# All value gathers as indirect transfers of GpSimd, registers read in one block, scratch in halves and block-diagonal V in place: block-sparse attention and a gated MLP

## The chip, the cores and the metric

The kernel runs on one core of one Trainium2 chip. The metric is device microseconds (us) of a run; most runs of one kernel on one chip lie within 1.5% of each other. A run is flagged slow when it is over 1.5% above the fastest of its kernel. The medians below are of all runs; the ratios leave out what was flagged slow within their rounds. The engines are called by the names of the profile: PE is TensorE, DVE is VectorE, ACT is ScalarE, POOL is GpSimd, SP is SyncE; "SPq" is the queue from which SyncE starts DMA transfers. The experiments ran on several chips, numbered here as the runs list them. Times are compared only with runs of the same kernels on the same chip, unless the text says that two chips are set side by side.

## The reference, cut to what matters

```python
# q, k, v: (4 batches, 8 heads, 768, 64) float32; blocks of 32 tokens; 24 blocks
mask = np.abs(blk_i - blk_j) <= 1                     # the window
mask |= first or last block, as query or as key       # the global blocks
for qb in range(24):
    for kb in sampled_blocks[qb]:                     # 3 random blocks each, known only at run time
        mask[qb*32:(qb+1)*32, kb*32:(kb+1)*32] = True
attn_out = softmax(where(mask, q @ k.T / 8, -1e9)) @ v
x = attn_out as (4, 768, 512)
u, v2 = split(gelu(x @ w_in)); v2 = layernorm(v2) * g_ln
out = x + (u * (w_sg @ v2 + b_sg)) @ w_out
```

What matters here is the random blocks. For each of 22 query blocks of each batch, 3 blocks of keys and 3 of values must be fetched by numbers that are in memory only.

## The kernel before

Each batch has 22 "value gathers", 88 in all: 96 rows of V for one query block, from a copy of V in DRAM (`scr`) to one of the slots of the tile `VR`. Two thirds of them are indirect transfers that GpSimd makes from row numbers in the tile `IDX`. Each third one is made of three ordinary transfers of SyncE, whose addresses come from registers.

```python
spset = list(range(2, 23, 3))          # the query blocks whose values SyncE gathers
...
if i in spset:
    def ga(e, i=i, rg=rg):
        if b == 0:
            load_regs(e, (0, 1, 2), "JSP", i)        # registers read just before use
            vals["SP", i] = vals["JSP"]
        return [e.dma_start(VR[32*j:32*j+32, rg, ...], src[bass.ds(vals["SP", i][j][0], 32), :]) for j in range(3)]
else:
    def ga(g, i=i, rg=rg):
        return g.indirect_dma_start(out=VR[0:96, rg, ...], in_=src[:, :],
                                    in_offset=bass.IndirectOffsetOnAxis(ap=IDX[0:96, i:i + 1], axis=0))
def kc(x, i=i, rg=rg):                               # the keys of the same blocks, copied on chip by VectorE
    if b == 0:
        load_regs(x, (0, 1), "JIT", i)               # just before use
        vals["DVE", i] = vals["JIT"]
    ...
```

The two global value blocks lie in `VG`, in each batch loaded whole by two transfers and then made block-diagonal by four fills of VectorE:

```python
for m in range(2):
    op("SP", f"vg{b}.{m}{hh}", ... ap(VG[bp], 64*m, 64, vo, [[1, w]]) <- whole rows ...)
def vones(x):
    x.memset(VG[bp][0:64, :, 64:65], 1.0)
    x.memset(VG[bp][64:128, :, 129:130], 1.0)
    x.memset(VG[bp][0:64, :, 65:130], 0.0)
    return x.memset(VG[bp][64:128, :, 0:65], 0.0)
```

An automatic list scheduler orders the operations of each engine by estimated times and priorities.

The softmax here doesn't subtract the row's maximum and nothing guards it: scores larger than these inputs give would overflow.

## Time and profile before

| | before |
|---|---|
| time, median of 3 runs | 299.96 us (298.42 to 302.66) |
| span of the profiled run, mean granted clock of PE | 294.7 us, 0.959 |
| PE busy, POOL busy | 223.0 us, 127.8 us |
| first attention matmul starts | 28.59 us |
| gathers of GpSimd, of SyncE | 60, 28 |

The first lines are of the page: busy time, share of the span, count of instructions.

```profile
PE 223.0 (76%) x3525; PEld 160.2 (54%) x3525; DVE 166.1 (56%) x480; ACT 149.4 (51%) x222; POOL 127.8 (43%) x224
...
PE 41%; DMA 15%; DVE 13%; POOL 10%; issue 8%; ACT 7%; SPq 3%; another core or an unknown queue 2%; DVEq 0%; ACTq 0%
```

No engine is full; the second line, the chain of waits by engine, passes through nearly all. The next lines are of the list of PE's waits (the longest, 8.8 us at the start, is among those left out): what PE was to run, what released it, us in total, times, the longest.

```profile
PE Ops L352 <- DVE VG L577: 5.3, 2, 4.4
...
PE Ops L352 <- issue: 4.5, 8, 1.2
PE Mps L352 <- DVE vh L874: 4.4, 2, 3.6
PE Mps L352 <- DVE VG L577: 4.1, 1, 4.1
...
PE Sps L352 <- issue: 2.8, 5, 1.1
```

The waits for `VG` and `vh` are what the change is after.

These two are of the groups of instructions (count, busy us and mean ns of one, then idle time before them) and of the waits of SyncE's queue.

```profile
L616 POOL DMA_INDIRECT VR<-scr,IDX x60 | 57.6, 960 | 35.1 <-PE Ops L352 13.6 <-issue 13.0 <-DMA scr<-VA 4.6
```

```profile
SPq L611 <- PE Ops L352: 32.9, 6, 14.5
```

A gather takes GpSimd about 0.92 us when it follows another, and 0.30 us pass between two. SyncE stands 33 us before its gathers until slots of `VR` are free. Last, VectorE's timeline at the start (start, duration, what, and the idle time before it):

```profile
9.09 0.18 DVE L423 CAST IDX<-Mps 96x24 int32<-96x24 f32 x1 [0.36 <-PE Mps L421]
19.61 0.49 DVE L584 MEMSET VA<- 32x520 bf16 x1 [10.35 <-DMA scr<-VA]
20.78 0.56 DVE L496 CAST qn<-x_tok 128x768 bf16<-128x768 f32 x1
```

VectorE idles 10.35 us there. This is the gap into which the change puts the reading of the registers.

### The profile page before, as it was taken

What the parts mean: (1) busy time and instruction counts of PE and PEld (TensorE: products, weight loads), DVE (VectorE), ACT (ScalarE), POOL (GpSimd) and SP (SyncE); (2) the same over time, 40 slices, a digit from 0 to 9 for tenths busy, and PEclk for the clock granted to TensorE, in tenths of its full rate; (3) what the DMA queues carried; (4) which work ended last, traced back from release to release, by engine and by line L of the source; (5) the groups of instructions that cost most, each with busy time, mean ns of one, the idle gap of its engine ahead of it and who ended that gap; (6) DMA issues with size and microseconds to landing.
All of it is one profiled execution on the core that took longest, in us unless ns stands there. A gap on an engine that the chain in (4) does not pass through costs nothing.

```text
span 294.7 us, 8583 instructions
## 1 busy us (share of the span) xinstructions
PE 223.0 (76%) x3525; PEld 160.2 (54%) x3525; DVE 166.1 (56%) x480; ACT 149.4 (51%) x222; POOL 127.8 (43%) x224
## 2 busy tenths in 40 slices
PE   0234569798899649597884897888868978999984
PEld 0123347576576327475662575666554766767542
DVE  7129432466746734335772875448646665556783
ACT  2760656783568103478554365684371755846100
POOL 1028455632643756632787547335880253003000
PEclk9999999869999989799999799999995999999999
DMA  8999686898768965596797177874830134030023
GB/s 155 266 277 245 166 260 155 185 219 212 167 135 190 265 178 140 144 259 151 168 252 172 42 144 185 173 183 148 270 110 1 29 91 127 6 110 0 0 108 108
DMA packets 87883, 45.66 MB, mean 155 GB/s; under 512 B 65924, under 2 KB 81700, under 8 KB 87844
## 3 DMA queue, kind: packets, MB, share of 16 engines
q1 hardware_dynamic: 83092, 34.79, 50.1%
q0 software_dynamic: 4752, 10.32, 13.5%
q8 instruction: 28, 0.46, 0.7%
q14 instruction: 11, 0.09, 0.1%
HBM read 36.76 MB, written 9.52 MB: 157 GB/s over the span
## 4 chain that ended last, share of the span: by engine, by line
PE 41%; DMA 15%; DVE 13%; POOL 10%; issue 8%; ACT 7%; SPq 3%; another core or an unknown queue 2%; DVEq 0%; ACTq 0%
PE Mps L352 21%; PE Ops L352 10%; PE Sps L352 7%; DMA ST<-in_v_dram 6%; POOL VR L616 5%; DMA ST<-in_q_dram 4%; PE Mps L842 3%; DVE gt L903 3%; DVE xg L906 2%; SPq L485 2%; DMA x_tok<-in_q_dram 2%; ACT PW L702 2%; ACT PR L701 2%; DMA uT<-in_k_dram 2%
## 5 line engine op out<-in xcount | busy, mean ns | idle before, releaser
L616 POOL DMA_INDIRECT VR<-scr,IDX x60 | 57.6, 960 | 35.1 <-PE Ops L352 13.6
L352 PE MATMUL Mps<-w_sgT,vh 128*128 128x384 bf16 x192 | 39.0, 351 | 11.7 <-DVE vh L874 4.4
L630 DVE COPY KR<-KT 128x128 bf16 x176 | 30.4, 232 | 19.3 <-issue 10.3
L701 ACT ACTIVATE PR<-Sps 96x1024 bf16<-96x1024 f32 (+1 forms) x24 | 22.8, 948 | 32.3 <-PE Sps L352 17.9
L634 POOL COPY KR<-KT 128x128 bf16 x88 | 24.1, 311 | 34.7 <-PE Sps L352 24.3
L702 ACT ACTIVATE PW<-Sps,b_odd 128x512 bf16<-128x512 f32 (+1 forms) x24 | 15.6, 649 | 33.6 <-PE Sps L352 21.1
L352 PEld LDWEIGHTS Mps<-w_sgT,vh 128*128 128x128 bf16 x192 | 17.9, 103 | 26.4 <-DVE VG L577 4.5
L903 DVE SCALAR_TENSOR_TENSOR gt<-Mps,gcol,bsg 128x384 f32<-128x384 f32 x32 | 19.7, 617 | 19.7 <-PE Mps L352 17.3
L352 PE MATMUL Mps<-w_out,xg 128*128 128x512 f32 x96 | 28.4, 426 | 2.4 <-DVE xg L906 1.6
L352 PE MATMUL Mps<-w_in,xg 128*128 128x512 f32 x96 | 26.7, 424 | 1.7 <-ACT QT L539 0.9
L352 PE MATMUL Mps<-xg,w_in 128*128 128x384 f32 x128 | 25.6, 352 | 3.0 <-ACT vg L861 1.8
L352 PEld LDWEIGHTS Mps<-xg,w_in 128*128 128x128 f32 x128 | 21.0, 188 | 7.6 <-ACT vg L861 2.9
L921 DVE TENSOR_TENSOR x_tok<-Mps,x_tok 128x512 f32<-128x512 f32 x24 | 16.5, 687 | 12.3 <-PE Mps L352 9.0
L352 PEld LDWEIGHTS Mps<-w_out,xg 128*128 128x128 f32 x96 | 16.9, 194 | 8.9 <-DVE xg L906 2.2
L845 ACT ACTIVATE xg<-Mps 128x512 fp32r<-128x512 f32 x24 | 14.3, 596 | 14.7 <-PE Mps L842 13.3
L352 PEld LDWEIGHTS Mps<-w_in,xg 128*128 128x128 f32 x96 | 17.4, 197 | 7.9 <-ACT vg L861 2.4
L352 PE MATMUL Ops<-VA,PW 128*64 128x65 bf16 x384 | 20.6, 206 | 1.5 <-issue 1.4
L861 ACT ACTIVATE vg<-Mps 128x512 f32<-128x512 f32 x24 | 13.9, 597 | 14.7 <-PE Mps L352 10.1
L888 ACT ACTIVATE uT<-Mps 128x384 f32<-128x384 f32 x32 | 15.7, 491 | 10.1 <-PE Mps L352 8.1
L352 PE MATMUL Ops<-VG,PG 128*128 128x130 bf16 x96 | 10.9, 238 | 12.6 <-DVE VG L577 5.3
L352 PEld LDWEIGHTS Ops<-VA,PW 128*64 128x64 bf16 x384 | 16.5, 119 | 6.2 <-issue 3.2
L863 DVE BATCH_NORM_STATS2 lnst<-vg 128x6 f32<-128x512 f32 x24 | 16.2, 677 | 6.0 <-ACT vg L861 5.9
(95 smaller groups left out, 392.5 us busy)
## 6 DMA issues: line engine op xcount, KB each, us to landing
out_dram<-x_tok SPq DMA_DIRECT2D x20, 256.0 KB, 3.5
ST<-in_k_dram SPq DMA_DIRECT2D x12, 384.0 KB
ST<-in_q_dram SPq DMA_DIRECT2D x12, 384.0 KB
ST<-in_v_dram SPq DMA_DIRECT2D x12, 384.0 KB
scr<-VA SPq DMA_DIRECT2D x4, 780.0 KB, 4.8
VR<-scr SPq DMA_DIRECT2D x84, 32.5 KB
VS<-scr SPq DMA_DIRECT2D x4, 650.0 KB
w_in<-in_moe_w_in_dram POOLq DMA_DIRECT2D x1, 2048.0 KB
```

Source lines behind the costliest of these rows:

```text
L352: return pe.matmul(o, l, r, start=start, stop=True, skip_group_check=True)
L616: return g.indirect_dma_start(out=VR[0:96, rg, v0:v1, :].rearrange("p h e -> p (h e)"), out_offset=None, in_=src[:, :], in_offset=bass.Ind ...
L630: ins = x.tensor_copy(KR[:, c0:c0 + n, rg, 32 * j:32 * j + 32], KT[:, c0:c0 + n, bass.ds(vals["DVE", i][j][0], 32)])
L634: op("POOL", f"kp{b}.{i}{hh}", lambda x, i=i, rg=rg: x.tensor_copy(KR[:, c0:c0 + n, rg, 64:96], KT[:, c0:c0 + n, bass.ds(vals["POOL"][0][i ...
L701: return lambda a: a.activation(o, i_, ACT.Exp, scale=SCALE)
L702: return lambda a: a.activation(o, i_, ACT.Exp, bias=bias[0:p1, 0:1], scale=SCALE)
L845: op("ACT", f"xE{b}.{tau}", lambda a: a.activation(xg[c][:, :, tc * P:tc * P + P], Mps[:, u.slot * 512:u.slot * 512 + 512].rearrange("p (a ...
L861: op("ACT", f"gV{b}.{tau}", lambda a: a.activation(vg[vr][:, :], Mps[:, u.slot * 512:u.slot * 512 + 512], ACT.Gelu_apprx_tanh), r=[("vp", ...
L863: op("DVE", f"bs{b}.{tau}", lambda x: x.bn_stats(lnst[:, vr, :], vg[vr][:, :]), r=[("vg", vr)], w=[("lnst", vr)], dur=0.73, prio=pr - 300)
L888: o = op("ACT", f"gU{b}.{c}{dt}", lambda a: a.activation(uT[c][:, dt, :], Mps[:, u.slot * 512:u.slot * 512 + 384], ACT.Gelu_apprx_tanh), r ...
L903: op("DVE", f"g1{b}.{c}{dt}", lambda x: x.scalar_tensor_tensor(gt[gr][:, :], Mps[:, u.slot * 512:u.slot * 512 + 384], gcol[:, dt:dt + 1], ...
L921: op("DVE", f"res{b}.{tau}", lambda x: x.tensor_tensor(x_tok[bp][:, tau, :], Mps[:, u.slot * 512:u.slot * 512 + 512], x_tok[bp][:, tau, :] ...
```

## The change

Its intent: take work off SyncE's queue and off VectorE's busy stretches. All 88 value gathers go to GpSimd. VectorE reads its 44 registers in one block in its idle time at the start. The copy of V to scratch goes in two halves, in batch 0 on ScalarE's queue. The zeros and ones of `VG` are set once for all, and transfers write only its diagonal. Some fills, evictions and orders of batch 0 move too. The diff, cut to its core:

```diff
-    spset = list(range(2, 23, 3))
+    spset = []
...
+    def regs_dve(x):
+        for i in range(1, 23):
+            load_regs(x, (0, 1), ("DVE", i), i)
+        return x.memset(lnt[0][:, :], 0.0)
+    op("DVE", "regsD", regs_dve, r=["IDX"], w=["regD", "lnt0"], dur=10.0, prio=-160)
...
             def kc(x, i=i, rg=rg):
-                if hh == 1 or b == 0:
-                    load_regs(x, (0, 1), "JIT", i)
-                if hh == 0 and b == 0:
-                    vals["DVE", i] = vals["JIT"]
...
-            hold["sc"] = op("SP", f"sc{b}.{hh}", ... dstr[0:768, :] <- VA ...)
+            for z in range(2):
+                o = op("ACT" if b == 0 else "SP", f"sc{b}.{z}", ... scr[0:768, 260 * z:260 * z + 260] <- VA[...4 * z:4 * z + 4...])
             for m in range(2):
-                op("SP", f"vg{b}.{m}{hh}", ... ap(VG[bp], 64 * m, 64, vo, [[1, w]]) ...)
-            def vones(x):                       # four fills of VG in each batch
+                op("SP", f"vg{b}.{m}", ... ap(VG[bp], 64 * m, 64, 65 * m, [[130, 4], [1, 64]]) ...)
...                                              # cut: fills of VG, VA at the start, table warm-up, batch 0's evictions
```

More of the change, by code (lines that the diff above doesn't have):

```diff
@@ L22 @@
 G2 = "DVE"
+EQA = 2
+XE0 = "DVE"
 ORD0 = "vkq"
@@ L357, in c_ident @@
     def c_ident(g):
+        g.memset(lnt[2][:, :], 0.0)
         g.memset(ident[:, :], 0.0)
         return g.memset(ident_f[:, :], 0.0)
-    op("POOL", "ident0", c_ident, w=["id0"], dur=0.4, prio=-200)
+    op("POOL", "ident0", c_ident, w=["id0", "lnt2"], dur=0.4, prio=-200)
     def c_ident1(g):
@@ L372, in bass_bigbird_attn__then__gmlp_full_block_kernel, with c_preV, c_preV1 @@
     op("POOL", "iota", c_iota, w=["iota"], dur=0.4, prio=-180)
+    def c_preV(vx):
+        ins = None
+        for i in range(2):
+            ins = vx.memset(VA[i][:, :, :, 64:65], 1.0)
+        return ins
+    op("DVE", "preV", c_preV, w=["preV"], dur=0.25, prio=-210)
+    def c_preV1(vx):
+        ins = None
+        for i in range(2):
+            vx.memset(VA[i][0:32, 0, :, 64:65], 0.0)
+            ins = vx.memset(VA[i][96:128, 5, :, 64:65], 0.0)
+        return ins
+    op("DVE", "preV1", c_preV1, r=["preV"], w=[("VA", i, h) for i in range(2) for h in range(4)], dur=0.3, prio=-205)
     def c_pre(vx):
@@ L377, in c_pre @@
         for i in range(2):
-            vx.memset(VA[i][:, :, :, 64:65], 1.0)
             vx.memset(KG[i][:, :, :], 0.0)
+            vx.memset(VG[i][:, :, :], 0.0)
         return vx.memset(KT[:, :, 768:800], 0.0)
-    op("DVE", "pre0", c_pre, w=["pre0"], dur=0.8, prio=-200)
+    op("DVE", "pre0", c_pre, w=["pre0"], dur=1.4, prio=-200)
     def c_pre1(vx):
@@ L386, in c_pre1 @@
         for i in range(2):
-            vx.memset(VA[i][0:32, 0, :, :], 0.0)
-            vx.memset(VA[i][96:128, 5, :, :], 0.0)
+            vx.memset(VG[i][0:64, :, 64:65], 1.0)
+            vx.memset(VG[i][64:128, :, 129:130], 1.0)
         vx.memset(PW[3][0:32, 0:520], 0.0)
@@ L391, in c_pre1, with dv @@
         return vx.memset(KR[:, :, :, 96:128], 0.0)
-    op("DVE", "pre1", c_pre1, r=["pre0"], w=["bias", "KTz"] + [("KG", i, c) for i in range(2) for c in range(4)] + [("VA", i, h) for i in range(2) for h in range(4)]
-       + [("KR", i, j, h) for i in range(NRING) for j in range(3) for h in range(2)] + ["PW3", "lnt3"], dur=1.2, prio=-190)
+    op("DVE", "pre1", c_pre1, r=["pre0"], w=["bias", "KTz"] + [("KG", i, c) for i in range(2) for c in range(4)]
+       + [("VG", i, m, c) for i in range(2) for m in range(2) for c in range(4)]
+       + [("KR", i, j, h) for i in range(NRING) for j in range(3) for h in range(2)] + ["PW3", "lnt3"], dur=1.6, prio=-190)
+    op("ACT", "warm", lambda a: a.activation(lnt[2][:, :], lnt[2][:, :], ACT.Exp), r=["lnt2"], w=["lnt2"], dur=1.6, prio=-200, mode="exp")
     op("SP", "sbi", lambda e: e.dma_start(sbi[:, :], sampled_blocks.bitcast(I32)), w=["sbi"], dur=0.6, prio=-300,
        dsem="c0", nbytes=600)
-    def dv(name, fn, r=(), w=(), dur=0.08, prio=-170):
+    def dv(name, fn, r=(), w=(), dur=0.17, prio=-170):
         op("DVE", name, fn, r=r, w=w, dur=dur, prio=prio)
@@ L418, in ixr @@
         return ins
-    dv("ix10", ixr, ["q3", "iota"], ["effr"], dur=0.25)
+    dv("ix10", ixr, ["q3", "iota"], ["effr"], dur=0.55)
     u_ix = Unit("M")
@@ L450, in d_scz @@
         return z
-    op("SP", "scz", d_scz, r=["PW3", ("PW", 3, 0), ("PW", 3, 1)], w=["scz"], dur=0.5, prio=-60, dsem="z0", nbytes=33000, nd=3 if SPLIT else 1)
+    op("ACT", "scz", d_scz, r=["PW3", ("PW", 3, 0), ("PW", 3, 1)], w=["scz"], dur=0.5, prio=-110, dsem="z0", nbytes=33000, nd=3 if SPLIT else 1)
     WP = -45
     def d_g(e):
+        for i in spset:
+            load_regs(e, (0, 1, 2), ("SP", i), i)
         with nc.allow_non_contiguous_dma(reason="tiny gain layout"):
@@ L458, in bass_bigbird_attn__then__gmlp_full_block_kernel @@
     hold = {"small": []}
-    op("SP", "gcol", d_g, w=["gcol"], dur=0.6, prio=WP, dsem="c1", nbytes=2e4)
+    hold["gcol"] = op("SP", "gcol", d_g, r=["IDX"], w=["gcol"], dur=5.3, prio=-92.5, dsem="c1", nbytes=2e4)
     hold["small"] += [op("SP", "bsg0", lambda e: e.dma_start(bsg[:, 0:736], moe_b_sg[32:768].partition_broadcast(P)), w=["bsg0"], dur=0.6, prio=WP, dsem="c2", nbytes=4e5)]
@@ L505, in loads @@
         for n_, (nm, c) in enumerate(od):
-            aft = [hold["sc"]] if hh else []
+            aft = []
             if b == 1:
@@ L511, in loads @@
             if b == 0 and nm == "q":
-                hold.setdefault("ldq", []).append(o)
+                o.seq.append(hold["gcol"])
+            if b == 0 and nm == "k":
+                hold["gcol"].seq.append(o)
     def transposes(b, hh):
@@ L529, in transposes @@
                 op("PE", f"TR{nm}{b}.{c}", tr, r=[(nm + "n", c), "ident"], w=[("trp", nm, b, c)], dur=0.42, prio=pr + c, mode="128", alloc=u, pre=tk)
-                ee = "ACT" if (nm == "q") == (b > 0) else "DVE"
+                ee = "ACT" if (nm == "q") == (b > 0) or (b == 0 and c >= EQA) else "DVE"
                 def ev(x, nm=nm, u=u, TT=TT, c=c, ee=ee):
@@ L558, in vprep @@
             vk = [("VA", bp, c) for c in hs]
-            dstr = scr if n == 4 else scrh[hh]
-            sk = "scr" if n == 4 else ("scrh", hh)
-            hold["sc"] = op("SP", f"sc{b}.{hh}", lambda e, dstr=dstr, c0=c0, n=n: e.dma_start(
-                dstr[0:768, :].rearrange("(t p) c -> p t c", p=P), VA[bp][:, :, 2 * c0:2 * c0 + 2 * n, :].rearrange("p t h e -> p t (h e)")),
-               r=vk, w=[sk], dur=0.5, prio=pr, dsem=f"sc{hh}", nbytes=199680 * n)
-            if b == 0 and hh == 0:
-                for o in hold["ldq"]:
-                    o.seq.append(hold["sc"])
@@ L567, in vprep @@
-            w = 130 * n
-            vo = 2 * c0 * 65
-            for m in range(2):
-                op("SP", f"vg{b}.{m}{hh}", lambda e, m=m, dstr=dstr, vo=vo, w=w: e.dma_start(
-                    ap(VG[bp], 64 * m, 64, vo, [[1, w]]), bass.AP(dstr.tensor, 0, [[736 * w, 2], [w, 32], [1, w]])),
-                   r=[sk], w=[("VG", bp, m, c) for c in hs], dur=0.5, prio=pr + 2, dsem=f"vg{m}{hh}", nbytes=66560)
-            def vones(x):
-                x.memset(VG[bp][0:64, :, 64:65], 1.0)
-                x.memset(VG[bp][64:128, :, 129:130], 1.0)
-                x.memset(VG[bp][0:64, :, 65:130], 0.0)
-                return x.memset(VG[bp][64:128, :, 0:65], 0.0)
@@ L578, in vprep @@
-            op("DVE", f"vo{b}.{hh}", vones, w=[("VG", bp, m, c) for m in range(2) for c in hs], dur=0.5, prio=pr + 2)
-            op("SP", f"vs{b}.{hh}", lambda e, dstr=dstr, vo=vo, w=w: e.dma_start(
-                ap(VS, 0, P, vo, [[520, 5], [1, w]]), bass.AP(dstr.tensor, 64 * w, [[w, P], [P * w, 5], [1, w]])),
-               r=[sk], w=[("VS", c) for c in hs], dur=0.5, prio=pr + 1, dsem=f"vs{hh}", nbytes=166400 * n)
-            def vz(x, c0=c0, n=n):
-                x.memset(VA[bp][0:32, 0, 2 * c0:2 * c0 + 2 * n, :], 0.0)
-                return x.memset(VA[bp][96:128, 5, 2 * c0:2 * c0 + 2 * n, :], 0.0)
@@ L586, in vprep @@
-            op("DVE", f"vz{b}.{hh}", vz, w=vk, dur=1.0, prio=pr + 2)
+            sk = [("scr", z) for z in range(2)]
+            for z in range(2):
+                o = op("ACT" if b == 0 else "SP", f"sc{b}.{z}", lambda e, z=z: e.dma_start(
+                    scr[0:768, 260 * z:260 * z + 260].rearrange("(t p) c -> p t c", p=P),
+                    VA[bp][:, :, 4 * z:4 * z + 4, :].rearrange("p t h e -> p t (h e)")),
+                    r=[("VA", bp, 2 * z), ("VA", bp, 2 * z + 1)], w=[("scr", z)], dur=0.65, prio=pr - 40, dsem=f"sc{z}{'a' if b == 0 else ''}", nbytes=399360)
@@ new lines, in vprep @@
+            for m in range(2):
+                op("SP", f"vg{b}.{m}", lambda e, m=m: e.dma_start(
+                    ap(VG[bp], 64 * m, 64, 65 * m, [[130, 4], [1, 64]]), bass.AP(scr.tensor, 65 * m, [[736 * 520, 2], [520, 32], [130, 4], [1, 64]])),
+                    r=sk, w=[("VG", bp, m, c) for c in hs], dur=0.7, prio=pr + 1, dsem=f"vg{m}", nbytes=131000)
+            op("SP", f"vs{b}", lambda e: e.dma_start(
+                ap(VS, 0, P, 0, [[520, 5], [1, 520]]), bass.AP(scr.tensor, 64 * 520, [[520, P], [P * 520, 5], [1, 520]])),
+               r=sk, w=[("VS", c) for c in hs], dur=0.6, prio=pr + 2, dsem="vs", nbytes=665600)
@@ L588, in bass_bigbird_attn__then__gmlp_full_block_kernel, with vz @@
+            def vz(x):
+                x.memset(ap(VA[bp], 0, 32, 0, [[1, 520]]), 0.0)
+                return x.memset(ap(VA[bp], 96, 32, 2600, [[1, 520]]), 0.0)
+            op("DVE", f"vz{b}.{hh}", vz, w=vk, dur=0.6, prio=pr + 2)
     rgof = {}
@@ L596, in gather @@
             pr = -20 + tau + 6 * hh
-        src = scr if n == 4 else scrh[hh]
-        sk = "scr" if n == 4 else ("scrh", hh)
+        src = scr
+        sk = [("scr", z) for z in range(2)]
         v0, v1 = 2 * c0, 2 * c0 + 2 * n
@@ L607, in ga @@
                 def ga(e, i=i, rg=rg):
-                    if b == 0:
-                        load_regs(e, (0, 1, 2), "JSP", i)
-                        vals["SP", i] = vals["JSP"]
                     return [e.dma_start(VR[32 * j:32 * j + 32, rg, v0:v1, :].rearrange("p h e -> p (h e)"),
                                         src[bass.ds(vals["SP", i][j][0], 32), :]) for j in range(3)]
-                ng_.append(op("SP", f"ga{b}.{i}{hh}", ga, r=[sk, "scz", "IDX"], w=vk, dur=2.8 if b == 0 else 1.9, prio=pr, dsem=f"vs{rg}h", nbytes=24960 * n, nd=3))
+                ng_.append(op("SP", f"ga{b}.{i}{hh}", ga, r=sk + ["scz", "IDX"], w=vk, dur=1.9, prio=pr, dsem=f"vs{rg}h", nbytes=24960 * n, nd=3))
             else:
@@ L617, in ga @@
                                                 in_offset=bass.IndirectOffsetOnAxis(ap=IDX[0:96, i:i + 1], axis=0))
-                ng_.append(op("POOL", f"ga{b}.{i}{hh}", ga, r=[sk, "scz", "IDX"], w=vk, dur=1.12, prio=pr, dsem=f"vs{rg}s", nbytes=24960 * n))
+                ng_.append(op("POOL", f"ga{b}.{i}{hh}", ga, r=sk + ["scz", "IDX"], w=vk, dur=1.12, prio=pr, dsem=f"vs{rg}s", nbytes=24960 * n))
             def kc(x, i=i, rg=rg):
                 ins = None
-                if hh == 1 or b == 0:
-                    load_regs(x, (0, 1), "JIT", i)
-                if hh == 0 and b == 0:
-                    vals["DVE", i] = vals["JIT"]
                 for j in range(2):
-                    if hh == 1:
-                        ins = x.tensor_copy(KR[:, c0:c0 + n, rg, 32 * j:32 * j + 32], KT[:, c0:c0 + n, bass.ds(vals["JIT"][j][0], 32)])
-                        continue
                     ins = x.tensor_copy(KR[:, c0:c0 + n, rg, 32 * j:32 * j + 32], KT[:, c0:c0 + n, bass.ds(vals["DVE", i][j][0], 32)])
@@ L632, in gather @@
             kk = [("KT", c) for c in hs] + ["KTz"]
-            op("DVE", f"kr{b}.{i}{hh}", kc, r=kk + ["IDX"], w=[("KR", rg, j, h) for j in range(2) for h in hk], dur=1.05 if b == 0 else 0.55, prio=pr)
+            op("DVE", f"kr{b}.{i}{hh}", kc, r=kk + ["regD"], w=[("KR", rg, j, h) for j in range(2) for h in hk], dur=0.55, prio=pr)
             op("POOL", f"kp{b}.{i}{hh}", lambda x, i=i, rg=rg: x.tensor_copy(
@@ L844, in mlp_x, with xev @@
         op("PE", f"xT{b}.{tau}", tr, r=[("x", bp, tau, 0), ("x", bp, tau, 1), "ident"], w=[("xp", b, tau)], dur=0.62, prio=pr, mode="128", alloc=u)
-        op("ACT", f"xE{b}.{tau}", lambda a: a.activation(
-            xg[c][:, :, tc * P:tc * P + P], Mps[:, u.slot * 512:u.slot * 512 + 512].rearrange("p (a c) -> p a c", c=P), ACT.Copy),
+        xe = XE0 if b == 0 else "ACT"
+        def xev(x):
+            o_, i_ = xg[c][:, :, tc * P:tc * P + P], Mps[:, u.slot * 512:u.slot * 512 + 512].rearrange("p (a c) -> p a c", c=P)
+            return x.tensor_copy(o_, i_) if xe == "DVE" else x.activation(o_, i_, ACT.Copy)
+        op(xe, f"xE{b}.{tau}", xev,
            r=[("xp", b, tau)], w=[("xg", c, tc)], dur=0.6, prio=pr, use=u)
```

## The prediction

> **What bounds it now.** The page shows TensorE busy for 223 of 294.7 us; no engine is near 100%. The windows of 10 us put TensorE's idle 72 us at about 24 before the first attention matmul (28.6 us), 8 in 30-60, and stalls at the heads of later batches. In the chain of waits and the timelines the change touches three:
> - batch 1, 103.7-108.1: 4.4 us on the memsets of VG, which wait behind two VG copies issued at 96.96 that seem to land near 107;
> - batch 2, 158.8-162.9: 4.1 us, same cause;
> - batch 3, 218.4-222.1: 3.6 us for vh, whose GpSimd part (lny) stands behind value gathers.
>
> The chain also runs through loads of q and v into ST (9%): the SyncE queue stands 33 us waiting for gather slots (waits of the DMA queue), with next-batch loads behind.
>
> **What changes.**
> 1. VG: the memsets (0.06+0.06+0.28+0.28 us, four times) go; the transfer writes only the diagonal. Matmuls wait for it alone; it is issued before VS, with no gathers behind it. It has 512 rows of 128 bytes instead of 128 of 1040. The Trainium skill ("DMA: Bandwidth & Descriptors", Specifications) puts line rate at 512 bytes or more; no run here shows what narrow rows cost. I expect it to land earlier anyway: TensorE gets back about 8.5 us.
> 2. All 28 SyncE gathers (84 DMAs) become GpSimd ones: 0.92 us busy + 0.30 us issue each, +34 us in all; busy 127.8 -> about 155 us. GpSimd has the room, but a refill of four slots takes 4.9 us in series instead of about 3: I charge 3.5 us of new waits. SyncE is free for loads, so q and v of batches 1-3 come several us earlier.
> 3. By the instruction order, lny of batches 1-3 now stands before the gathers: 3.6 us come back in batch 3.
> 4. Registers: 44 loads in one block on VectorE. Before, two loads cost the 0.60 us gap before each pair of KR copies (22 times, 13 us); in the block I expect 0.30 each, 13 us, from about 8.5 to 21.5 us, where VectorE idled 10.35 us. But q's casts stand behind it, so the first attention matmul comes at 27-30 us, hardly before today's 28.6.
> 5. Scratch in halves on ScalarE's queue: first gather about 2 us earlier (19.7 -> 17.5).
> 6. Batch 0: x evictions move to VectorE (+3.6 us); ScalarE has one pair of table loads less (2 x 1.28 us). w_in is issued after 16 gathers instead of 8 (32.6 -> about 40 us) and may hold the first w_in matmuls up to 3 us.
>
> **Sum.** Gains 8.5 (VG) + 3.6 (vh) + 2 (batch 0) + 2 (loads); costs 3.5 (serial gathers) + 1.5 (w_in). Net -11 us: **289 us**, 8 in 10 within **281 to 297**. Faster by over 2%: 0.76; within 2%: 0.20; slower: 0.04.
>
> **Signs.** No memset of VG after the start; no TensorE wait for it over 1 us; GpSimd about 155 us busy with 88 gathers; no SyncE wait for gather slots; first attention matmul at 27-30 us; register block about 13 us; TensorE busy near 223 us.
>
> **What would make it wrong.** Serial gathers holding the value matmuls (releaser shown as unknown queue) or the casts behind them; the narrow VG transfer landing as late as before; the register block lasting well over 13 us and delaying q. Or the reverse: early loads closing more of the 20-odd us of load waits on the chain, giving 280 or less.

## More of the kernel before

The attention itself is many short matmuls (`Sps<-QT,KR`, 32 columns; `Sps<-QT,KT`, 64; `Ops<-VA,PW` and `Ops<-VR,PR`, 65), each with a weight load of its own.

The lines with "issue" are idle time in which PE waited for nothing that the profile shows. All such lines of this kernel together come to 9.1 us.

## The result, and the profile after

The changed kernel took **345.79 us** (median of 4 runs, 343.2 to 347.03), beside 299.28 us for the kernel before (4 runs). The ratio of the fast runs is 1.152, with a 95% interval of 1.141 to 1.163. Such a ratio, here and below, is the mean time of one kernel's fast runs over that of the other's of the same rounds, so it isn't quite the ratio of the medians quoted. The prediction of 289 us, 281 to 297, was wrong: the change made the kernel 15% slower.

The page's line of busy times, and the chain by engine:

```profile
PE 240.2 (70%) x3525; PEld 171.4 (50%) x3525; DVE 164.7 (48%) x475; ACT 146.5 (43%) x217; POOL 151.9 (44%) x253
...
PE 47%; issue 14%; DVE 13%; ACT 7%; DMA 7%; DVEq 5%; POOL 3%; another core or an unknown queue 2%; SPq 0%; ACTq 0%; POOLq 0%
```

PE has the same 3525 matmuls but is busy 17 us longer: the mean granted clock fell from 0.959 to 0.871. PE's waits, longest first:

```profile
PE Sps L354 <- issue: 18.1, 24, 2.5
PE Ops L354 <- issue: 17.6, 22, 2.3
PE Mps L556 <- DVE qn L524: 10.5, 1, 10.5
```

The wait for `vh` is gone and that for `VG` is down to 0.8 us, as predicted. In their place stand 38.9 us of "issue" (all lines together, 9.1 before), and all but 3.2 us of that before the short matmuls of attention. Where do they lie? First GpSimd, then PE, in the same stretch of batch 1:

```profile
120.65 0.92 POOL L633 DMA_INDIRECT VR<-scr,IDX  x1 [0.30 <-issue]
121.87 0.92 POOL L633 DMA_INDIRECT VR<-scr,IDX  x1 [0.30 <-issue]
...
126.78 0.92 POOL L633 DMA_INDIRECT VR<-scr,IDX  x1 [0.30 <-issue]
```

```profile
123.97 0.29 PE L354 MATMUL Ops<-VA,PW 128*64 128x65 bf16 x2 [0.51 <-issue]
125.36 0.21 PE L354 MATMUL Ops<-VA,PW 128*64 128x65 bf16 x1 [1.10 <-issue]
126.07 0.32 PE L354 MATMUL Ops<-VA,PW 128*64 128x65 bf16 x2 [0.49 <-issue]
...
130.34 1.48 PE L354 MATMUL Ops<-VA,PW 128*64 128x65 bf16 x23 [0.50 <-issue]
```

Twelve gathers follow each other from 113 to 127.7 us, with 0.3 us between two. From 121.8 us on PE gets one to three matmuls, then nothing for half a microsecond or more, though the profile shows nothing that it waits for. 2.6 us after the last gather, 23 matmuls run at once. The same picture stands in the gather runs of batches 2 and 3. We call this starving.

The group of gathers and the start of VectorE:

```profile
L633 POOL DMA_INDIRECT VR<-scr,IDX x88 | 82.3, 935 | 59.1 <-PE Ops L354 25.4 <-issue 21.4 <-DMA scr<-VA 9.2
```

```profile
8.20 0.18 DVE L443 CAST IDX<-Mps 96x24 int32<-96x24 f32 x1 [0.36 <-PE Mps L441]
27.04 0.06 DVE L464 MEMSET lnt<- 128x2 f32 x1 [18.66 <-issue]
...
29.09 0.58 DVE L524 CAST qn<-x_tok 128x768 bf16<-128x768 f32 x1
```

The 44 register reads took 18.66 us, 0.42 us each, not 13. The first cast of q came at 29.1 us instead of 20.8, and the first attention matmul at 35.54 us instead of 28.59. SyncE no longer waits for slots (the 32.9 us are gone).

So 7.0 us were lost before the first attention matmul. The other 42.7 us (344.3 - 35.54 against 294.7 - 28.59) were lost after it.

### The profile page after: what moved, and what is told of

It reads as the page before. It is cut to its first block, busy times and chain, and to the rows that moved or that the text cites. A ratio compares the mean times of both kernels' runs of the same rounds, so it can differ in the third digit from the quotient of the medians.

```text
span 344.3 us, 8390 instructions
## 1 busy us (share of the span) xinstructions
PE 240.2 (70%) x3525; PEld 171.4 (50%) x3525; DVE 164.7 (48%) x475; ACT 146.5 (43%) x217; POOL 151.9 (44%) x253
## 4 chain that ended last, share of the span: by engine, by line
PE 47%; issue 14%; DVE 13%; ACT 7%; DMA 7%; DVEq 5%; POOL 3%; another core or an unknown queue 2%; SPq 0%; ACTq 0%; POOLq 0%
PE Mps L354 21%; PE Ops L354 12%; PE Sps L354 8%; DVEq L455 5%; PE Mps L852 4%; DMA ST<-in_v_dram 2%; PE Mps L556 2%; DMA ST<-in_q_dram 2%; ACT PR L711 2%; DVE gt L917 2%; DMA VG<-scr 2%; DVE KR L640 1%; DVE xg L920 1%; ACT PW L712 1%
## 5 line engine op out<-in xcount | busy, mean ns | idle before, releaser
L633 POOL DMA_INDIRECT VR<-scr,IDX x88 | 82.3, 935 | 59.1 <-PE Ops L354 25.4
L354 PE MATMUL Mps<-w_sgT,vh 128*128 128x384 bf16 x192 | 41.0, 362 | 3.6 <-issue 1.7
L917 DVE SCALAR_TENSOR_TENSOR gt<-Mps,gcol,bsg 128x384 f32<-128x384 f32 x32 | 19.7, 617 | 42.7 <-PE Mps L354 28.0
L354 PE MATMUL Sps<-QT,KT 64*128 64x64 bf16 x544 | 19.5, 209 | 20.0 <-issue 13.8
L354 PE MATMUL Ops<-VA,PW 128*64 128x65 bf16 x384 | 24.2, 217 | 8.9 <-issue 8.6
L354 PE MATMUL Mps<-w_in,xg 128*128 128x512 f32 x96 | 28.7, 443 | 2.2 <-ACT QT L569 0.9
L712 ACT ACTIVATE PW<-Sps,b_odd 128x512 bf16<-128x512 f32 (+1 forms) x24 | 15.6, 649 | 32.0 <-PE Sps L354 31.9
L354 PEld LDWEIGHTS Sps<-QT,KT 64*128 64x128 bf16 x544 | 13.0, 104 | 26.7 <-issue 17.8
L354 PEld LDWEIGHTS Ops<-VA,PW 128*64 128x64 bf16 x384 | 19.1, 129 | 14.2 <-issue 11.5
L833 DVE RECIPROCAL rden<-Ops 128x8 f32<-128x8 f32 x24 | 4.9, 203 | 39.1 <-PE Sps L354 21.6
L569 ACT ACTIVATE QT<-Mps 128x768 bf16<-128x768 bf16 x14 | 11.7, 841 | 24.8 <-issue 12.7
L711 ACT ACTIVATE PW<-Sps 128x1024 bf16<-128x1024 f32 x12 | 11.9, 1020 | 23.7 <-remote 20.3
```

The source lines that it names most:

```text
L354: return pe.matmul(o, l, r, start=start, stop=True, skip_group_check=True)
L569: return x.activation(o_, src, ACT.Copy) if ee == "ACT" else x.tensor_copy(o_, src)
L633: return g.indirect_dma_start(out=VR[0:96, rg, v0:v1, :].rearrange("p h e -> p (h e)"), out_offset=None, in_=src[:, :], in_offset=bass.Ind ...
L711: return lambda a: a.activation(o, i_, ACT.Exp, scale=SCALE)
L712: return lambda a: a.activation(o, i_, ACT.Exp, bias=bias[0:p1, 0:1], scale=SCALE)
L917: op("DVE", f"g1{b}.{c}{dt}", lambda x: x.scalar_tensor_tensor(gt[gr][:, :], Mps[:, u.slot * 512:u.slot * 512 + 384], gcol[:, dt:dt + 1], ...
```

## The experiments

At the outset, **theory A** said that runs of GpSimd gathers starve PE of short matmuls, on any chip. **Its rivals** were other parts of the change, above all the register block. The first call undid one part at a time. (The expectations name theories by letters; A is the same throughout, and the letters from the third call on are defined where they first stand.)

### Call 1, chip 14: one part undone, one part alone

`a1_spgather` puts a third of the gathers back on SyncE, `a2_jitregs` puts the registers back to their first use, `a12_both` undoes both. `b1_allpool` is the kernel before with all gathers on GpSimd and nothing else.

```diff
# a1, against the changed kernel (and its registers read just before use, as before)
-    spset = []
+    spset = list(range(2, 23, 3))
# a2, against the changed kernel
-    op("DVE", "regsD", regs_dve, ...)
+                if b == 0: load_regs(x, (0, 1), "JIT", i); vals["DVE", i] = vals["JIT"]
# b1, against the kernel before
-    spset = list(range(2, 23, 3))
+    spset = []
```

> The changed kernel with the 28 SyncE gathers given back to SyncE (registers read just in time there). Theory A (long unbroken runs of GpSimd gathers starve TensorE's small attention matmuls of instructions): 300 to 312 us; TensorE's idle put down to 'issue' falls from 39 us to about 10, the late start of 35.5 us stays. Theory B (values arrive too late because gathers are serial): also about 305, but then TensorE's waits for VR would be what vanishes, and they were only 0.7 us. Theory C (the register block and the new order of batch 0 cost the time): stays above 335.

> The changed kernel with the register block on VectorE undone (two loads just in time before each pair of KR copies of batch 0, as before). Theory A: start of attention back from 35.5 to about 28 us, the rest unchanged: 336 to 342 us. Theory C: 300 us or less.

> Both undone, all else of the change kept (diagonal VG, scratch halves on ScalarE, table warm-up, x evictions on VectorE). Theory A: 290 to 298 us, a little faster than before, as the 8.5 us of VG waits are gone. Theory C would give the same here, so this run tells whether the kept parts are a gain: above 302 they are not.

> The kernel before with nothing changed but all 88 value gathers on GpSimd. Theory A: 325 to 345 us, with 'issue' waits of TensorE at 30 us or more against 9 before. Theory B: slower too, with TensorE or its exps waiting for VR. Theory C: 296 to 303 us.

| chip 14 | gathers of GpSimd | median us | ratio to before, 95% |
|---|---|---|---|
| before | 60 | 283.74 | |
| a1_spgather | 60 | 287.78 | 1.012 (1.005 to 1.020) |
| a2_jitregs | 88 | 285.44 | 1.002 (0.992 to 1.011) |
| a12_both | 60 | 280.22 | 0.988 (0.980 to 0.996) |
| b1_allpool | 88 | 288.43 | 1.019 (1.010 to 1.029) |

Theory A's numbers for `a2` and `b1` failed by 37 us and more: with all 88 gathers on GpSimd neither starved (3.9 and 0.4 us of "issue" on PE). But the register block didn't fit either, for `a1` keeps it and didn't starve. (Two of `b1`'s four runs are flagged slow, 290.51 and 290.22, and its ratio contains them. Its two fast runs, 282.45 and 286.64, have a mean of 1.003 of before's.) What stood out was the kernel before: 284 us here, 299 in the first comparison, and the same program. Two things could be at work: either the undone parts only starve PE together, or the chip matters.

`b1` bears on one side of the prediction. It has all gathers on GpSimd but the old `VG`, and the waits for `VG` stay: 9.5 us, beside 5.3 + 4.1 = 9.4 in the kernel before. So it is the new `VG`, not the moved gathers, that shortens them:

```profile
PE Ops L352 <- DVE VG L577: 9.5, 4, 3.7
```

### Call 2, chip 1: probes of fixed loads

Two programs with wrong output, with one loaded stretch after another: 800 short matmuls (64 columns, each with its weight load) alone, then beside 12 gathers of GpSimd, and so on.

> A probe, wrong results on purpose: one engine works through a fixed stream while another does one thing, phase after phase with a barrier between. Streams: 800 small matmuls (64x128 by 64x64) or 90 large (128x128 by 128x512) on TensorE, 200 tiny copies on VectorE, 100 tiny activations on ScalarE. Beside: nothing; 12 GpSimd gathers of 96 rows of 1040 bytes back to back; 36 SyncE transfers of the same bytes; 12 direct GpSimd transfers of the same bytes; 12 GpSimd memsets; gathers each followed by a memset; gathers of 64-byte rows. Theory A: the small-matmul phase takes over 1.5 times as long beside back-to-back gathers, about 1.0 times beside SyncE transfers and memsets; the large-matmul phase within 1.1. If descriptor writing is what disturbs, direct GpSimd transfers and the 64-byte gathers disturb as much as the wide ones; if it is the moved data, SyncE transfers disturb too and narrow gathers do not. Theory B: no phase of TensorE changes by more than 5%.

> The same probe: 800 small matmuls written out, and 800 in a loop of 16 [...], each alone and beside 12 gathers; then written out beside 2, 4 and 8 gathers. If the fetch of instructions is what starves, the loop takes no longer beside gathers than alone while the written-out stream does; if records or semaphores are what stalls, both slow down. Against the number of gathers: a stall that starts only after 3 to 4 gathers (as in the trace after) shows as no loss at 2 and a growing one at 8 and 12.

In both, no stretch was starved: 800 matmuls took 21.3 us alone and 22.7 beside 12 gathers in `m1`, 20.7 and 22.4 in `m2`. `m2`'s loop of 16 instructions took 22.2 alone and 30.8 beside gathers, with 1.8 us of idle; in the kept traces the granted clock of the second was 0.57 on average, against 1.00 alone. (The kept traces of `m1` and `m2` are of a second execution. Its stretches are within 1.5 us of those given here.) Chip 1 did not starve (before: 286.69 us, one run, state unknown), so they told nothing of the cause. They did become the measure for the other kind of chip.

### Call 3, chip 12: the changed kernel itself

No edit in `c_after`. `c_a2` and `c_a1` repeat `a2` and `a1`.

> The changed kernel itself, unedited, on the chip that this call lands on. Theory A as it stands (runs of GpSimd gathers starve PE of its small matmuls whenever all 88 gathers are on GpSimd): ratio to before 1.13 to 1.17 again, with over 30 us of PE waits of the form 'issue'. Theory B (starvation needs this chip or this placement as well; elsewhere the change costs only its register block, about 7 us, and its serial gathers, about 5 us, less 3.5 us for what it keeps): ratio 1.02 to 1.04 and under 6 us of 'issue' waits on PE. Theory C (the two undone parts interact: register block and all-GpSimd gathers together starve PE, each alone does not): ratio 1.10 or more on the chip where the two single undoings stay under 1.03.

> The changed kernel with its register block undone (registers read where first used, as before), all gathers still on GpSimd; a repeat beside the changed kernel. Theory A and B on a chip that starves: ratio to before 1.10 to 1.15, about 7 us under the changed kernel. B on a chip that does not: 0.99 to 1.02. Theory C: under 1.03 while the changed kernel is over 1.10 on the same chip.

> The changed kernel with a third of the gathers back on SyncE's queue, register block kept; a repeat beside the changed kernel. Theory A and B on a chip that starves: ratio 1.01 to 1.04, that is 30 us or more under the changed kernel. B on a chip that does not: 1.00 to 1.02, about 5 us under it. Theory C: under 1.03 while the changed kernel is over 1.10 on the same chip.

| chip 12 | median us | ratio to before, 95% |
|---|---|---|
| before | 283.07 | |
| c_after | 280.98 | 0.989 (0.982 to 0.996) |
| c_a2 | 282.17 | 0.997 (0.989 to 1.006) |
| c_a1 | 287.82 | 1.016 (1.008 to 1.023) |

**The unchanged text of the changed kernel took 281 us here and 346 in the first comparison.** On this chip it is 1% faster than the kernel before. That ends theory C (that the parts do it together) and the rivals of the first call: nothing in the program alone makes it 15% slower. Theory B of this call, that starving needs the chip as well, had its "issue" right (under 6 us) but not its ratio, 1.02 to 1.04; and it had `c_a1` about 5 us under the changed kernel, where it was 6.8 us over. (`c_a2`'s ratio contains one run flagged slow, 283.98.) Beside the profile of the first comparison, the lines of `c_after`:

```profile
PE 219.8 (78%) x3525; PEld 161.3 (58%) x3525; DVE 166.7 (59%) x475; ACT 145.9 (52%) x217; POOL 153.0 (55%) x253
...
L633 POOL DMA_INDIRECT VR<-scr,IDX x88 | 82.9, 942 | 39.6 <-issue 22.2
```

```profile
PE Mps L556 <- DVE qn L524: 11.7, 2, 10.8
...
PE Ops L354 <- DMA VR<-scr,IDX: 2.9, 3, 1.9
...
PE Mps L556 <- issue: 1.3, 1, 1.3
```

The same 88 gathers at the same 0.94 us, the same bytes, the same late start (first attention matmul at 35.77 us). But "issue" on PE is 1.3 us, not 38.9. The spans differ by 344.3 - 280.4 = 63.9 us: 37.6 of these are the "issue" waits, and 20.4 the longer busy time of PE. The longer busy time goes with the lower granted clock: 240.2 x 0.871 = 209 and 219.8 x 0.945 = 208. Why the clock was lower is not shown.

### Call 4, chip 15: a chip that starves

> The changed kernel unedited, once more on whatever chip this call lands on. It has been 346 us beside a before of 299 on the chip of the comparison, and 281 beside 283 on another chip, with the same instructions. Theory B (the starving is a trait of some chips, and shows already in the kernel before): if the kernel before takes 297 to 303 here, the changed kernel takes 335 to 350 with over 30 us of PE waits of the form 'issue'; if before takes 281 to 288, it takes 279 to 285 with under 6 us of them. Theory G (a passing state of that one session, not of the chip): the two need not go together.

> The changed kernel with a third of its gathers back on SyncE. Where the changed kernel starves (335 to 350 us): theory A, that unbroken runs of GpSimd gathers do it, expects 300 to 312 us here; theory F, that such a chip is slow at feeding PE whatever GpSimd does, expects 335 us or more. Where it doesn't starve: 285 to 290, about 2.5% over the changed kernel, as on the two chips before.

> The probe of fixed loads again (wrong output on purpose): stretches of 800 small matmuls alone, beside 12 GpSimd gathers, beside SyncE transfers, beside gathers spaced by fills. On the chip of its first run the stretches took 21 to 25 us each. Theory A on a chip that starves: alone about 21.5 us as there, beside unbroken gathers 26 us or more, beside spaced gathers or SyncE transfers under 25. Theory F there: the stretch alone is already over 24 us. On a chip that doesn't starve: the numbers of the first run within 1 us.

This call landed on a chip where the kernel before took 300.4 us, as in the first comparison.

| chip 15 | median us | ratio to before, 95% |
|---|---|---|
| before | 300.40 | |
| d_after | 345.54 | 1.151 (1.143 to 1.159) |
| d_a1 | 313.67 | 1.045 (1.035 to 1.054) |

The 15% came back to the tenth of a per cent, so it is no passing accident of one session (theory G):

```profile
PE Sps L354 <- issue: 19.5, 19, 5.0
PE Ops L354 <- issue: 18.4, 26, 2.3
```

All "issue" lines of `d_after` come to 44.6 us. Putting 28 of the 88 gathers back on SyncE brought them to 15.6 and gave 31.9 us of the time back. The 313.67 us are within 2 us of theory A's range of 300 to 312; theory F, that such a chip feeds PE slowly whatever GpSimd does, wanted 335 or more. On chip 12 the same edit cost 6.8 us.

The probe told it most plainly. From first to last matmul of a stretch of 800, us:

| stretch | chip 1 | chip 15 |
|---|---|---|
| alone | 21.3 | 21.0 |
| beside 12 gathers of GpSimd | 22.7 | **36.2** |
| beside 36 plain transfers of SyncE | 24.9 | 25.4 |
| beside 12 plain transfers of GpSimd | 23.2 | 21.7 |
| beside 12 fills of GpSimd, 1 us each | 21.6 | 24.1 |
| beside 12 gathers with a 1 us fill after each | 21.2 | 23.1 |
| beside 12 gathers of 64-byte rows | 22.2 | **35.2** |

Windows of 5 us in the second stretch, one of chip 1 and then two of chip 15 (window: its length, busy us and count of PE, PEld, DVE, ACT, POOL; then clock, DMA share, GB/s):

```profile
36.00:41.00 5.00, 2.37 (x151) 2.15 (x143) 0.00 (x0) 0.00 (x0) 3.78 (x5) 1.00 0.33 86
```

```profile
36.00:41.00 5.00, 1.40 (x18) 0.79 (x18) 0.00 (x0) 0.00 (x0) 3.78 (x5) 0.50 0.33 85
41.00:46.00 5.00, 0.82 (x10) 0.46 (x9) 0.00 (x0) 0.00 (x0) 3.78 (x5) 0.50 0.32 85
```

GpSimd does exactly the same on both (3.78 us busy, 5 gathers), and the DMA engines move the same. PE gets 10 to 18 matmuls through instead of 150. So it isn't the traffic: 64-byte rows, a sixteenth of the bytes, cost the same, and transfers of SyncE cost nothing more than elsewhere. (The 12 plain transfers of GpSimd are a shorter load than the gathers: they keep it busy for 6.1 us, the gathers for 11.2.) The granted clock was 0.50 in those windows. What sets it isn't shown: it was 0.50 as well in `m3`'s loop on chip 1 with PE busy 4.88 of 5 us.

Nor is it PE alone. VectorE's 200 tiny copies took 15.2 us beside gathers on chip 1 and 23.0 on chip 15 (14.6 alone there). ScalarE's 100 took 10.4 and 13.6.

A stretch of 90 long matmuls (512 columns) took 19.2 us beside gathers on both chips. That doesn't prove them immune: each starved stretch begins with about 55 matmuls at full speed, before the drip, and the gathers' 14.6 us hold only about 68 long ones, which start every 0.21 us.

### Call 5, chip 1 again: a gap between gathers

`e_gap` puts a fill before each gather. `m3` is a second probe, with a loop and with several gaps.

```diff
                 def ga(g, i=i, rg=rg):
+                    g.wait_ge(FS, fc[0]); g.memset(FZ[:, :], 0.0).then_inc(FS, 1); fc[0] += 1   # FZ: 128 x 512
                     return g.indirect_dma_start(...)
```

> The changed kernel with one addition: before each of its 88 gathers GpSimd fills a small unused tile (about 0.5 us), so that no gather follows another directly. Instruction order otherwise the same. If the kernel before takes 297 to 303 us here (a chip that starves): theory A (the unbroken run) expects 290 to 312 us and under 12 us of PE waits of the form 'issue'; theory D (the number of gathers) expects 340 us or more. If before takes 281 to 288 here: both expect 279 to 292, and the run only tells what the 45 us of fills on GpSimd cost.

> A second probe (wrong output on purpose): 800 small matmuls each time, alone; beside 12 unbroken gathers; as a loop of 16 instructions, alone and beside 12 gathers; beside gathers with a 0.1 us fill after each, a 0.5 us fill after each, a 1 us fill after each second, after each fourth; beside 4 and 8 gathers; alone. On a chip that starves: straight code beside 12 gathers 33 to 38 us against 21 alone. Theory I: the loop takes the same beside gathers as alone, 20 to 24 us at the full clock (up to 31 at half clock, with under 2 us of idle). Theory X: the loop is stretched with over 6 us of idle. Theory A: 0.5 us fills 22 to 25 us, 4 gathers in a row under 25 us, 8 about 29, 12 about 36. On another chip all straight stretches within 21 to 25 us.

Chip 1 did not starve this time either. `e_gap` took 314.74 us, far outside the 279 to 292 expected. The fast runs of before took 278.9 us (no interval is given for so few). Nothing starved; GpSimd had become the bound:

```profile
PE Ops L357 <- DMA VR<-scr,IDX: 26.5, 10, 4.3
```

```profile
POOL 42%; DMA 21%; PE 12%; DVE 8%; issue 6%; DVEq 5%; ACT 4%; POOLq 0%; ACTq 0%
```

Another 47.6 us of GpSimd work (88 fills of 0.54 us) cost over 30 us beside the kernel before; the changed kernel itself was not run on this chip. So even where nothing starves, the all-GpSimd gathers leave no such room, though the engine is busy only 55% of the time (`c_after`): the gathers come in four bursts, one for each batch. `m3` gave the values of a free chip; they stand in the next table.

### Call 6, chip 0: the same probe on a chip that starves

`f_m3` is `m3` again. `f_tiny` is `e_gap` with a fill of 128 x 16, 0.13 us.

> The changed kernel with a very short fill (128 x 16, about 0.1 us) before each of its 88 gathers; order of instructions otherwise the same. Where the kernel before takes 281 to 288 us: 279 to 288 (the 0.5 us fills had cost 33 us there because PE then waited for the gathers; 0.1 us each should fit into the pause of 0.3 us between gathers). Where before takes 297 to 303: if any break of the run cures, 290 to 305 with under 12 us of PE waits of the form 'issue'; if a gap has to be wide, 335 to 350 as without fills.

> The second probe again. Where before takes 297 to 303: straight code beside 12 unbroken gathers 33 to 38 us against 21 alone; theory I (delivery of new instructions): the loop beside gathers has under 2 us of idle on PE, as alone; theory X: over 6 us. Fills of 0.5 us bring the straight code to 22 to 26 us; 4 gathers in a row cost under 4 us, 8 about 8. Where before takes 281 to 288: all straight stretches 21 to 25 us, as on the chip before.

Here before took 300.79 us: a chip that starves. `f_tiny` took 345.61 us, ratio 1.151 (1.142 to 1.159), with 39.0 us of "issue": a gap of 0.1 us cures nothing. The probe, from first to last matmul, us:

| stretch of 800 matmuls | chip 1 (m3) | chip 0 (f_m3) |
|---|---|---|
| alone, first and last | 20.7, 21.6 | 20.8, 21.6 |
| 4, 8, 12 gathers | 22.6, 22.4, 22.2 | 24.6, 30.2, 34.7 |
| 12 gathers, 0.1 us fill after each | 22.2 | 36.0 |
| 12 gathers, 0.5 us fill after each | 22.5 | 30.1 |
| 12 gathers, 1 us fill after each second, each fourth | 22.1, 24.3 | 29.4, 35.8 |
| loop of 16, alone | 22.1 | 22.2 |
| loop of 16, beside 12 gathers (mean granted clock 0.57 and 0.56) | 30.8 | 44.9 |

Two of our theories fell or had to be mended here.

**Theory I fell.** It said that the delivery of new instructions from memory is held up, so that a loop, which repeats 16 instructions, would be spared, with under 2 us of idle. The loop starved as well:

```profile
L88 PE MATMUL Sps<-QT,KT 64*128 64x64 bf16 x800 | 32.1, 233 | 13.1 <-issue 11.9
```

On chip 1 the same loop had 1.6 us of idle. The traces also hold the packets that bring instructions from memory (`--dma`, kind "instruction", 16 KB each), which we hadn't asked about. In straight code on chip 1 four came from 32 to 47 us (`m1`'s kept trace). In `m3`'s loop beside gathers none came from 76 to 106 us, in the starved loop of `f_m3` one from 88 to 133: a loop needs almost no delivery. And in the straight code of chip 15 (`d_m1`) none came from 36 to 51 us. PE ran 25 matmuls from 36.8 to 48.7 us and then 91 from 48.8 to 51.2, so their instructions had been delivered while it stood.

That theory X's number (over 6 us) held doesn't make execution itself slow: a matmul lasts 0.19 us at the full clock on either chip. What is held up lies between the delivered instruction and its start, whether it is new or repeated. Where, the profile doesn't show.

**It doesn't take an unbroken run.** Theory A expected 22 to 26 us with fills of 0.5 us; it was 30.1. In the stretch with a 1 us fill after each second gather, PE falls in step with GpSimd (first PE's timeline, then GpSimd's):

```profile
206.24 1.47 PE L124 MATMUL Sps<-QT,KT 64*128 64x64 bf16 x48 [0.46 <-issue]
208.04 0.36 PE L124 MATMUL Sps<-QT,KT 64*128 64x64 bf16 x6 [0.33 <-issue]
208.79 0.35 PE L124 MATMUL Sps<-QT,KT 64*128 64x64 bf16 x6 [0.40 <-issue]
209.56 1.36 PE L124 MATMUL Sps<-QT,KT 64*128 64x64 bf16 x44 [0.41 <-issue]
```

```profile
207.90 0.92 POOL L60 DMA_INDIRECT VR<-scr,IDX  x1 [0.30 <-issue]
208.82 0.97 POOL L132 MEMSET MB<- 128x1024 f32 x1
209.94 0.93 POOL L60 DMA_INDIRECT VR<-scr,IDX  x1 [0.16 <-issue]
```

Two drips of 5 or 6 matmuls, then some 45 at full speed, over and over. The pattern repeats every 3.3 us, and so does GpSimd's, two gathers and a fill. The fast stretch at 209.56 begins 0.7 us after the fill does and ends 1.1 us after it. So PE is held back while GpSimd makes a gather, and fed again while it doesn't, about a microsecond late. The loss, against the mean of 21.2 us alone, is about 0.9 us for each of 4 gathers and 1.1 us for each of 8 or 12. A gap after each or each second gather helps by about its own length: with 1 us after each, the stretch on chip 15 lost only about 2 us. A gap after each fourth gave nothing (35.8), as did 0.1 us. And `e_gap`, 314.74 us even where nothing starves, has shown that the kernel can't afford gaps of half a microsecond.

### Call 7, chip 10: fewer gathers on GpSimd

The last question was whether a version is left that beats both kernels. `g_a12` repeats `a12_both`; `g_half` also puts half of the gathers on SyncE.

```diff
# g_half, against a12_both
-    spset = list(range(2, 23, 3))
+    spset = list(range(1, 23, 2))
```

> The changed kernel with half of its gathers (44 of 88) back on SyncE and the register block undone. Where the kernel before takes 297 to 303 us: at about 1 us of PE time for each gather beside small matmuls, 280 to 292, ratio to before 0.93 to 0.975. Where before takes 279 to 288: 277 to 288, ratio 0.98 to 1.01; SyncE's transfers take over 80 us of its queue, which may delay loads.

> The changed kernel with a third of its gathers (28 of 88) back on SyncE and the register block undone; a repeat of the best version on the first chip (ratio 0.988 there). Where before takes 297 to 303: 294 to 304, ratio 0.98 to 1.01, since it has as many GpSimd gathers as before. Where before takes 279 to 288: ratio 0.98 to 1.00.

This was again a chip that starves (before 300.67; four of its seven runs are flagged slow, and the fast ones took 296.01 to 299.28). `g_half` took 301.4 us, ratio 1.012 (1.002 to 1.022), and `g_a12` 303.81, ratio 1.020 (1.009 to 1.030). Both missed: `g_half` was expected at 280 to 292, and `g_a12`, within its 294 to 304 us, at a ratio of 1.01 at most. Taking 16 more gathers away brought "issue" on PE only from 12.1 to 10.7 us, and a new wait took part of the gain:

```profile
PE Ops L354 <- DMA VR<-scr: 7.3, 1, 7.3
```

That is PE waiting once for a gather of SyncE; SyncE's queue is 14% of the chain in this kernel. "One microsecond for each gather" is thus no rule for the kernel: it holds in the probe, where PE has only short matmuls to do. What a gather costs in the kernel depends on what PE had to do beside it.

### All of it, by kind of chip

| kernel | GpSimd gathers | chips 12, 14, 1 | chips 15, 0, 10 and the first |
|---|---|---|---|
| before | 60 | 283.07, 283.74 | 299.28 to 300.79 |
| changed | 88 | 280.98 | 345.79, 345.54 |
| changed, 0.1 us fills | 88 | | 345.61 |
| registers as before (a2) | 88 | 285.44, 282.17 | |
| before, all gathers on GpSimd (b1) | 88 | 288.43 | |
| a third back on SyncE (a1) | 60 | 287.78, 287.82 | 313.67 |
| both undone (a12) | 60 | 280.22 | 303.81 |
| both undone, half on SyncE (g_half) | 44 | | 301.40 |
| changed, 0.5 us fills | 88 | 314.74 | |

No version beat both kernels by 2% on either kind of chip. On a starving chip the kernel before is still the best tried.

## Why the prediction was wrong

**The step that failed** is point 2 of the prediction: "GpSimd has the room, but a refill of four slots takes 4.9 us in series instead of about 3: I charge 3.5 us of new waits." It counted only how long the gathers take and who waits for their data. That wait stayed small, as charged (0.7 us of PE waiting for `VR` in the changed kernel of the first comparison, 2.9 on chip 12). What it left out is what a gather does to the other engines while it runs. On the chip of the comparison the changed kernel shows 38.9 us of "issue" on PE, and a mean granted clock of 0.871. On chip 12 the same program, with the same gathers, shows 1.3 us and 0.945, and takes 281 us. On a starving chip, 28 gathers put back on SyncE gave 31.9 us back, and the probe shows the cost of a gather by itself.

**The trace of before had the sign.** It has 9.1 us of "issue" on PE. It also has waits labelled as for another core or an unknown queue, 9.8 us of ScalarE and 6.7 us of VectorE in all, up to 4.3 us each, beside runs of three gathers. None of the kept traces of the first calls' free chips (`c_after`, `b1`, `a1`, `a2`, `a12`, `c_a1`, `c_a2`) has such a wait. The kernel before was starving too: 300 us on chips of this kind, 283 on the others, a difference of 17 us that no step of the prediction asked about. (No trace of it on a free chip was kept; that the whole 17 us are starving is argued.)

**The register block** was mis-sized (point 4). Predicted: 0.30 us for each read, 13 us, from 8.5 to 21.5 us, first attention matmul at 27 to 30. Measured: 0.42 us, 18.66 us, from 8.4 to 27.0, first attention matmul at 35.5. That is 7.0 us later than before, on chip 12 as well (35.8). What it costs at the end isn't settled. With a third of the gathers on SyncE it costs 7.5 us (a1 against a12, chip 14). With all on GpSimd it shows no cost (c_after against c_a2, chip 12: 281.0 and 282.2). Why the late start is made good there was not found.

**What was right.** The waits for `VG` fell from 9.4 us to 0.8 (0.2 on chip 12); the wait for `vh` in batch 3 is gone (with a third of the gathers back on SyncE it is there again, 1.2 us in `c_a1` and 5.8 in `d_a1`); SyncE doesn't wait for slots; GpSimd is busy 151.9 us with 88 gathers (about 155 predicted). The narrow `VG` transfer, with rows of 128 bytes, holds PE up little in these two (in `a2`, 3.3 us). Here the Trainium skill, "DMA: Bandwidth & Descriptors", Specifications, puts line rate at 512 bytes or more; no run compares the narrow rows with wide ones, so what they cost is not shown. The first gather came at 21.45 us, neither at 17.5 nor as early as before (19.75): point 5 gained nothing.

**The size on a free chip.** Even without starving the prediction was too bright: a ratio of 0.989 against 289/299.96 = 0.963. The gap, 2.6% or about 7 us, is as large as the lateness of the start. That the one makes up the other is an argument, not shown.

**What stays open.** What differs between the chips, and what in a gather holds the other engines up. That instructions lie delivered and aren't begun (call 6) narrows the second down, no more. Six chips: three starved (0, 10, 15), three didn't (1, 12, 14). The first comparison's chip isn't numbered; its times are of the starving kind. No numbered starving chip was met twice, so there the chip and the session can't be told apart. All that is shown is that it goes with the chip as far as seen, hits PE, VectorE and ScalarE, comes and goes with each indirect gather of GpSimd, and not with plain transfers of GpSimd or SyncE, nor with bytes. All listed runs were recorded ones; whether it is there without recording can't be told from them.

## What to carry to other kernels

Idle time marked "issue" on an engine that has ready work is not noise: find out what runs beside it before you move more of that onto the chip. An engine's busy share doesn't tell what its instructions do to the others; a probe of some hundred short matmuls, alone and beside the suspect, shows it in one run. Before explaining a surprise by the program, run the same unchanged kernel once more elsewhere: here 65 us of a 346 us kernel depended on the chip, and the same change was 1% faster on another.

## What the Trainium skill lacked or had wrong

- "SBUF — State Buffer", Who interferes with whom, says of SBUF ports: "PE and ACT never wait on anyone." As a guide to what overlapping costs this was not enough. On chips 15 and 0, 800 short matmuls took 36.2 and 34.7 us beside 12 gathers of GpSimd, against 21 alone, and 100 short ScalarE instructions 13.6 against 10.4. No run shows that ports are the way in which it happens, so the sentence itself isn't disproved. No page tells of engines being fed slowly while GpSimd makes an indirect transfer, nor that chips differ in this.
- "Runtime: NRT & Kernel Launch", Instruction fetch mechanics, has instructions streamed in blocks of 256, the cost "mostly hidden". Straight code of short matmuls agrees with the block: alone it runs 128 matmuls with their 128 weight loads, then stops for 1.3 to 1.7 us. But it isn't hidden there: 7.1 of 21.3 us on chip 1. A loop of 16 has no such stops (2.0 us of idle in 22.1).
- "Perfetto Trace Analysis", DMA Instruction — SWDGE (GPSIMD), says that a GpSimd transfer's bar ends when its descriptors are written, not when the data have moved. The trace agrees: 0.92 us of bar, 3.9 us from issue to landing (median, `c_after`). What the page lacks is what that bar costs others: about 1.1 us of PE's short matmuls for each gather of a run on a starving chip (36.2 us for 800 beside 12, against 21.0 alone), little on the other kind (22.7 against 21.3).
- Some pages give figures for other loads of registers; none gives the cost of reading one from on-chip memory on VectorE: 0.42 us each in a block of 44 here.
